# Agent attention with a max-out layer: keys and queries transposed by DMA, SBUF to SBUF, instead of by TensorE and VectorE

## The chip, the cores and the metric

The kernel runs on one core of a Trainium2 chip. The metric is device microseconds (us) of one execution. Shapes: q, k and v are 4 x 12544 x 128 in float32, the agents are 4 x 49 x 128, the output is 50176 x 128 in float32.

## The reference

```python
scale = 1.0 / np.sqrt(q.shape[-1])
def sm(a, b):
    s = scale * (a @ b.transpose(0, 2, 1))
    s = s - s.max(-1, keepdims=True)
    e = np.exp(s)
    return e / (e.sum(-1, keepdims=True) + 1e-09)
agent_v = sm(agents, k) @ v              # 49 x 128 for each batch
x = (sm(q, agents) @ agent_v)            # 12544 x 128 for each batch
x = x.reshape(B * S, D)
h = np.maximum(np.maximum(x @ w1, x @ w2), x @ w3)   # 768 hidden columns
out = h @ w_out
```

## The kernel before, in words

A batch has 12544 rows, cut into 13 groups: twelve of 8 x 128 rows and one of 2 x 128. Row t0 + p·n + j of a group lies on partition p, column block j. Every group of every batch is worked twice: once as a **k group** (keys and values, which build the agent values), and, when all k groups of its batch are done, as a **q group** (queries, hidden layer, output). The k groups of batch b+1 run beside the q groups of batch b; the k groups of batch 0 run alone at the start, and the q groups of batch 3 alone at the end.

**A k group.** `load` (L141) brings k and v in, 512 KB each, by two DMAs on the SP queue. `cast` (L148) turns both to bf16 on POOL (v on ACT in batch 0). `transposes` (L157) turns eight 128x128 blocks of keys on TensorE into the PSUM tile `m_ps`, and `evacuate` (L162) copies that to SBUF as `kT` on VectorE. `scores` (L166) multiplies `kT` by the agents, `exps` (L173) takes the exponential on ACT, `values` (L177) multiplies by the values and by ones, `accumulate` (L187) adds the result to `Eacc` on VectorE. After the last group `k_tail` (L207) normalises and multiplies by the three weight matrices, so that the hidden layer later takes the exponentials of the queries directly.

**A q group.** `load`, `cast`, `transposes` (L256), `evacuate` (L263) as above, with `qT` as result; `scores` (L267) and `exps` (L273) give the exponentials `e_q`. Then for each f of six slices of 128 hidden columns: `first` (L303) multiplies one weight difference, `relu_first` (L306) applies ReLU on ACT (into `a_sb`, or in place for the last slice, L309), `second` (L314) multiplies the other, and `max_second` (L317) takes the maximum of both on VectorE (L323; ACT for the last slice, L321). Products go to PSUM tiles `uv_ps`, of which there are three. `out_linear` (L325) and `out_hidden` (L332) form the output in PSUM (`o_ps`), `out_scale` (L340, line L344) divides by the sums of the exponentials on VectorE, and `store` (L349) writes it out on the SP queue.

**PSUM.** `uv_ps` takes six banks, `o_ps` one, `m_ps` one. All of the transposes, scores, values, sums and the products of `k_tail` go through that one `m_ps` bank, one after the other.

**Order.** The order is written by hand. Each step of a group is put down by `at(key + offset, step)`, six units of key being one group; all steps are sorted by key and issued in that order, and each engine and each DMA queue works in that order. So in the middle batches one turn of six units holds one k group and one q group of every stage. Of the steps that the change touches:

```python
        at(key - 20, load)         # k and q groups
        at(key - 12, cast)
        at(key - 0.6, transposes)  # k group, with key counted one group later
        at(key - 0.1, evacuate)
        at(key + 0.65, scores)
        at(key - 3.0, transposes)  # q group
        at(key - 2.6, evacuate)
        at(key - 1.75, scores)
```

SP's queue holds all large transfers: loads of q, k and v and the store, in the order of their keys; a waiting store holds up the loads behind it.

Of the kernel before, what the change touches and what calls it, by code (L numbers as in the profile page):

```python
# [10 lines left out]
BF16 = mybir.dt.bfloat16  # L11
# [5 lines left out]
def kernel(  # L17
# [18 lines left out]
    nc = tc.nc  # L36
    B, N, C = q.shape
    A = agents.shape[1]
    Dff = moe_w1.shape[1]
    scale = 1.0 / math.sqrt(C)  # L40
    P = 128
    NF = Dff // P
    H = 64
    GT = 8
# [5 lines left out]
    NG = len(sizes)  # L50
# [4 lines left out]
    work = ctx.enter_context(tc.tile_pool(name="work", bufs=2))  # L55
# [8 lines left out]
    def m_tile(dtype=FP32):  # L64
        return psum.tile([P, 512 if dtype == FP32 else 1024], dtype, tag="m", bufs=1, name="m_ps")
# [3 lines left out]
    def at(key, fn):  # L69
        ops.append((key, len(ops), fn))  # L70


    ident = const.tile([P, P], BF16, name="ident")
# [3 lines left out]
    agT = const.tile([P, B, H], BF16, name="agT")  # L77
# [9 lines left out]
    for i, w in enumerate((moe_w1, moe_w2, moe_w3)):  # L87
        t = const.tile([P, Dff], FP32, name=f"wst{i}")
# [42 lines left out]
    LEAD = 1  # L131
# [4 lines left out]
    def k_group(b, g):  # L136
        n, t0 = sizes[g], starts[g] * P
        key = 6.0 * (NG * (b - 1) + g - LEAD)
        d = {}

        def load():  # L141
            for name, src in (("k", k), ("v", v)):
                t = loads.tile([P, GT, C], FP32, tag=f"{name}_st", bufs=3, name=f"{name}_st")
                nc.sync.dma_start(t[:, :n, :],
                                  src[b, t0:t0 + n * P, :].rearrange("(p j) c -> p j c", j=n))
                d[name] = t

        def cast():  # L148
            d["kb"] = work.tile([P, GT, C], BF16, tag="k_bf", name="k_bf")
            nc.gpsimd.tensor_copy(out=d["kb"][:, :n, :], in_=d["k"][:, :n, :])  # L150
            d["vb"] = work.tile([P, GT, C], BF16, tag="v_bf", bufs=3, name="v_bf")
            if b == 0:
                nc.scalar.activation(d["vb"][:, :n, :], d["v"][:, :n, :], AF.Copy)
            else:
                nc.gpsimd.tensor_copy(out=d["vb"][:, :n, :], in_=d["v"][:, :n, :])  # L155

        def transposes():  # L157
            t = d["kT_ps"] = m_tile(BF16)
            for j in range(n):
                nc.tensor.transpose(t[:, j * P:(j + 1) * P], d["kb"][:, j, :], ident)  # L160

        def evacuate():  # L162
            d["kT"] = work.tile([P, GT * P], BF16, tag="kT", name="kT")
            nc.vector.tensor_copy(out=d["kT"][:, :n * P], in_=d["kT_ps"][:, :n * P])  # L164

        def scores():  # L166
            t = d["s"] = m_tile()
            sumtile["t"] = t
            for j in range(n):
                nc.tensor.matmul(t[:, j * A:(j + 1) * A], d["kT"][:, j * P:(j + 1) * P], agT[:, b, :A],  # L170
                                 start=(j == 0), stop=True, skip_group_check=True)

        def exps():  # L173
            d["e"] = work.tile([P, GT * A], BF16, tag="e_k", name="e_k")
            nc.scalar.activation(d["e"][:, :n * A], d["s"][:, :n * A], AF.Exp, scale=scale)  # L175

        def values():  # L177
            t = d["s"]
            c = GT * A
            for j in range(n):  # L180
                e = d["e"][:, j * A:(j + 1) * A]
                nc.tensor.matmul(t[:, c:c + A], d["vb"][:, j, :], e, start=False, stop=True,  # L182
                                 skip_group_check=True)
                nc.tensor.matmul(t[:, c + A:c + 2 * A], ones, e, start=False, stop=True,  # L184
                                 skip_group_check=True)

        def accumulate():  # L187
            c = GT * A
            if g == 0:
                Eacc[b] = work.tile([P, 2 * A], FP32, tag="Eacc", name="Eacc")  # L190
                nc.vector.tensor_copy(out=Eacc[b], in_=d["s"][:, c:c + 2 * A])
            else:
                nc.vector.tensor_tensor(out=Eacc[b], in0=d["s"][:, c:c + 2 * A], in1=Eacc[b],  # L193
                                        op=ALU.add)

        at(key - 20, load)
        at(key - 12, cast)
        at(key - 0.6, transposes)
        at(key - 0.1, evacuate)
        at(key + 0.65, scores)  # L200
        at(key + 1.35, exps)
        at(key + 2.3, values)
        at(key + 2.75, accumulate)
        if g == NG - 1:
            k_tail(b, key + 2.8)

    def k_tail(b, key):  # L207
        d = {}

        def normalise():  # L210
            E = Eacc[b]
            r = work.tile([P, A], FP32, tag="k_recip", name="k_recip")
            nc.vector.reciprocal(r, E[:, A:2 * A])
            d["avT"] = work.tile([P, H], BF16, tag="avT", name="avT")
            nc.vector.memset(d["avT"], 0.0)
            nc.vector.tensor_tensor(out=d["avT"][:, :A], in0=E[:, :A], in1=r, op=ALU.mult)
            G[b] = work.tile([P, WC], BF16, tag="G", name="G")

        def product(i):
            c0, c1 = i * 512, min((i + 1) * 512, WC)  # L220
            t = m_tile()
            for h in range(2):

                c = c0 + (C if c0 >= C1O and h == 0 else 0)
                nc.tensor.matmul(t[h * H:(h + 1) * H, :c1 - c0], d["avT"], wall[:, c:c + c1 - c0],  # L225
                                 start=True, stop=True, skip_group_check=True)
            if i % 2:
                nc.vector.tensor_copy(out=G[b][:, c0:c1], in_=t[:, :c1 - c0])
            else:
                nc.scalar.activation(G[b][:, c0:c1], t[:, :c1 - c0], AF.Copy)  # L230

        at(key, normalise)
        for i in range(-(-WC // 512)):
            at(key + 0.02 * (i + 1), lambda i=i: product(i))


    def q_group(b, g):
        n, t0 = sizes[g], starts[g] * P
        nh = n // 2
        T = nh * P  # L240
        pairs = [range(0, min(2, nh)), range(2, nh)]
        key = 6.0 * (NG * b + g)
        d = {}
# [10 lines left out]
            nc.gpsimd.tensor_copy(out=d["qb"][:, :n, :], in_=d["q"][:, :n, :])  # L254

        def transposes():  # L256
            t = d["qT_ps"] = m_tile(BF16)
            for j in range(n):
                jj, h = divmod(j, 2)
                i = h * nh + jj  # L260
                nc.tensor.transpose(t[:, i * P:(i + 1) * P], d["qb"][:, j, :], ident)  # L261

        def evacuate():  # L263
            d["qT"] = work.tile([P, GT * P], BF16, tag="qT", name="qT")
            nc.vector.tensor_copy(out=d["qT"][:, :n * P], in_=d["qT_ps"][:, :n * P])  # L265

        def scores():  # L267
            t = d["s"] = m_tile()
            for h in range(2):
                nc.tensor.matmul(t[h * H:(h + 1) * H, :T], agT[:, b, :], d["qT"][:, h * T:(h + 1) * T],  # L270
                                 start=True, stop=True, skip_group_check=True)

        def exps():  # L273
# [77 lines left out]
            nc.sync.dma_start(out[row:row + n * P, :].rearrange("(p j) c -> p j c", j=n),  # L351
                              d["out"][:, :n, :])

        at(key - 20, load)
        at(key - 12, cast)
        at(key - 3.0, transposes)
        at(key - 2.6, evacuate)
        at(key - 1.75, scores)
        at(key - 1.3, exps)
        at(key + 2.05, sums)  # L360
# [16 lines left out]
            at(e + scaled, lambda o=o: out_scale(o))  # L377
        at(e + 6.3, store)

    at(-6.0 * (NG + LEAD) - 21, prep)  # L380
    at(-6.0 * (NG + LEAD) + 12, prep_weights)
    for b in range(B):
        for g in range(NG):
            k_group(b, g)
            q_group(b, g)
# [34 lines left out]
```

## Time and profile before

| | us |
|---|---|
| median of 3 runs | 686.89 |
| lowest and highest of them | 685.15, 694.22 |
| the profiled execution's own time | 681.0 |
| its span, first to last instruction | 679.2 |

The span is the stretch in which instructions run; 1.8 us of the execution lie around it. Times in the trace count from its start. An engine's busy time is a sum over its instructions; whether it bounds a stretch is read from the waits there. In the rows PE is TensorE's matmul side, PEld its weight loads, DVE is VectorE, ACT ScalarE, POOL GpSimd, and SPq the queue of DMA issues on SyncE. Three stretches have a different make-up: the k groups of batch 0 alone (to about 70 us), the three batches with k and q groups, and batch 3's q groups alone (from about 540 us).

### The profile page before, as it was taken

How to read it: one execution, taken by the hardware profiler on the slowest of the kernel's cores; microseconds unless marked ns; L12 is line 12 of the kernel's file. 1: busy time of each engine (PE TensorE's matmuls, PEld its weight loads, DVE VectorE, ACT ScalarE, POOL GpSimd, SP SyncE). 2: the span in 40 equal slices, each digit the busy share in tenths (PEclk: the TensorE clock that was granted, in tenths of full speed). 3: DMA queues.
4: the chain of work that ended last, by engine and by line, in shares of the span. 5: the costliest groups of instructions: out<-in, count | busy, mean ns of one | idle time of the engine just before them, and what ended most of it. 6: DMA issues, size and time to landing. Idle time of an engine off the chain costs nothing.

```text
span 679.2 us, 14666 instructions
## 1 busy us (share of the span) xinstructions
PE 524.7 (77%) x6104; PEld 324.2 (48%) x6104; DVE 446.0 (66%) x603; ACT 416.8 (61%) x493; POOL 140.3 (21%) x149
## 2 busy tenths in 40 slices
PE   1555498888887778888888778888888778888886
PEld 1444245545544445554554445455555444555454
DVE  1322267676767478676778467677777467877875
ACT  2332166767676376767667366766667467777774
POOL 2123332322212132222213122222310011101000
PEclk9999999999999699999999699999999699999999
DMA  9767723463536273364445283354312131322111
GB/s 338 260 252 274 268 86 126 147 226 125 177 128 217 91 288 126 126 225 149 149 155 188 95 293 128 145 199 174 119 63 101 63 126 63 125 94 94 71 64 71
DMA packets 31438, 105.39 MB, mean 155 GB/s; under 512 B 3399, under 2 KB 6411, under 8 KB 31371
## 3 DMA queue, kind: packets, MB, share of 16 engines
q1 hardware_dynamic: 29952, 102.77, 42.3%
q10 hardware_dynamic: 1419, 1.67, 0.7%
q8 instruction: 48, 0.79, 0.5%
q14 instruction: 19, 0.16, 0.1%
HBM read 78.74 MB, written 25.69 MB: 154 GB/s over the span
## 4 chain that ended last, share of the span: by engine, by line
PE 56%; DVE 17%; ACT 10%; issue 6%; DVEq 0%; POOL 0%; ACTq 0%
PE o_ps L337 19%; PE uv_ps L298 17%; ACT a_sb L312 8%; DVE r L323 7%; PE o_ps L328 5%; DVE o_sb L344 5%; PE m_ps L261 5%; PE m_ps L160 3%; PE m_ps L270 2%; DVE kT L164 2%; DVE recips L290 1%; PE m_ps L182 1%; PE m_ps L225 1%; PE m_ps L184 1%; PE m_ps L170 1%
## 5 line engine op out<-in xcount | busy, mean ns | idle before, releaser
L312 ACT ACTIVATE a_sb<-uv_ps 128x1024 bf16<-128x1024 f32 (+1 forms) x260 | 251.3, 974 | 113.1 <-PE uv_ps L298 110.3
L323 DVE TENSOR_TENSOR r<-uv_ps,a_sb 128x1024 bf16<-128x1024 f32 (+1 forms) x260 | 295.0, 1157 | 26.5 <-PE uv_ps L298 17.8
L298 PE MATMUL uv_ps<-e_q,G 49*128 49x512 bf16 (+1 forms) x1248 | 212.8, 383 | 54.3 <-ACT a_sb L312 44.1
L337 PE MATMUL o_ps<-wo_bf,r 128*128 128x128 bf16 x2352 | 179.1, 224 | 0.0
L337 PEld LDWEIGHTS <-r 128*128 128x128 bf16 x2352 | 140.5, 100 | 53.4 <-issue 50.8
L298 PEld LDWEIGHTS <-G 49*128 49x128 bf16 x1248 | 60.1, 94 | 119.8 <-issue 84.0
L254 POOL CAST q_bf<-q_st 128x1024 bf16<-128x1024 f32 (+1 forms) x52 | 51.6, 993 | 299.7 <-issue 174.7
L164 DVE COPY kT<-m_ps 128x1024 bf16<-128x1024 bf16 (+1 forms) x52 | 34.4, 661 | 100.7 <-PE m_ps L160 100.7
L150 POOL CAST k_bf<-k_st 128x1024 bf16<-128x1024 f32 (+1 forms) x52 | 51.6, 992 | 203.8 <-PE m_ps L160 186.6
L344 DVE TENSOR_TENSOR o_sb<-o_ps,recips 128x512 f32<-128x512 f32 (+1 forms) x100 | 66.7, 667 | 27.4 <-PE o_ps L337 27.4
L309 ACT ACTIVATE uv_ps<-uv_ps 128x1024 f32<-128x1024 f32 (+1 forms) x52 | 49.9, 959 | 28.0 <-DVE r L323 23.4
L328 PE MATMUL o_ps<-G,e_q 128*128 128x256 bf16 x196 | 39.7, 283 | 32.1 <-DVE o_sb L344 32.1
L321 ACT ACTIVATE r<-uv_ps 128x1024 bf16<-128x1024 f32 (+1 forms) x52 | 50.7, 975 | 17.9 <-PE uv_ps L298 17.8
L175 ACT ACTIVATE e_k<-m_ps 128x392 bf16<-128x392 f32 (+1 forms) x52 | 24.9, 479 | 53.5 <-PE m_ps L170 53.2
L182 PE MATMUL m_ps<-e_k,v_bf 128*128 128x49 bf16 x392 | 30.5, 194 | 15.7 <-ACT e_k L175 15.7
L328 PEld LDWEIGHTS <-e_q 128*128 128x128 bf16 x196 | 12.3, 97 | 62.6 <-DVE o_sb L344 44.0
L160 PE MATMUL m_ps<-ident,k_bf 128*128 128x128 bf16 x392 | 37.5, 250 | 6.0 <-DVE Eacc L193 4.1
L265 DVE COPY qT<-m_ps 128x1024 bf16<-128x1024 bf16 (+1 forms) x52 | 34.3, 660 | 11.2 <-PE m_ps L261 9.8
L155 POOL CAST v_bf<-v_st 128x1024 bf16<-128x1024 f32 (+1 forms) x39 | 38.8, 994 | 0.0
L261 PE MATMUL m_ps<-ident,q_bf 128*128 128x128 bf16 x392 | 31.3, 223 | 9.3 <-DVE Eacc L193 6.2
L261 PEld LDWEIGHTS <-q_bf 128*128 128x128 bf16 x392 | 24.2, 99 | 22.4 <-issue 21.3
L160 PEld LDWEIGHTS <-k_bf 128*128 128x128 bf16 x392 | 30.2, 113 | 8.7 <-issue 8.6
(49 smaller groups left out, 269.6 us busy)
## 6 DMA issues: line engine op xcount, KB each, us to landing
k_st<-in_k_dram SPq DMA_DIRECT2D x48, 512.0 KB, 5.3
v_st<-in_v_dram SPq DMA_DIRECT2D x48, 512.0 KB, 5.8
q_st<-in_q_dram SPq DMA_DIRECT2D x48, 512.0 KB, 4.4
out_dram<-o_sb SPq DMA_DIRECT2D x48, 512.0 KB, 3.0
wst<-in_moe_w_dram ACTq DMA_DIRECT2D x3, 384.0 KB, 8.3
k_st<-in_k_dram SPq DMA_DIRECT2D x4, 128.0 KB, 4.2
v_st<-in_v_dram SPq DMA_DIRECT2D x4, 128.0 KB, 3.6
q_st<-in_q_dram SPq DMA_DIRECT2D x4, 128.0 KB, 2.8
```

The source lines that it names most:

```text
L150: nc.gpsimd.tensor_copy(out=d["kb"][:, :n, :], in_=d["k"][:, :n, :])
L160: nc.tensor.transpose(t[:, j * P:(j + 1) * P], d["kb"][:, j, :], ident)
L254: nc.gpsimd.tensor_copy(out=d["qb"][:, :n, :], in_=d["q"][:, :n, :])
L261: nc.tensor.transpose(t[:, i * P:(i + 1) * P], d["qb"][:, j, :], ident)
L298: nc.tensor.matmul(t[:, h, :T], G[b][h * H:h * H + A, col + f * P:col + (f + 1) * P], d["e"][h * H:h * H + A, :T], start=start, stop=True, ...
L309: nc.scalar.activation(u, u, AF.Relu)
L312: nc.scalar.activation(a_sb[f][:, :, :T], u, AF.Relu)
L321: nc.scalar.activation(r[:, :, :T], u, AF.Relu)
L323: nc.vector.tensor_tensor(out=r[:, :, :T], in0=u, in1=a_sb[f][:, :, :T], op=ALU.max)
L328: nc.tensor.matmul(t[:, i * 2 * C:(i + 1) * 2 * C], d["e"][:, jj * P:(jj + 1) * P], G[b][:, C1O:C1O + 2 * C], start=(i == 0), stop=False, ...
L337: nc.tensor.matmul(t[:, c:c + C], r_sb[f][:, h, jj * P:(jj + 1) * P], wo_bf[:, f, :], start=False, stop=(f == NF - 1), skip_group_check=True)
L344: nc.vector.tensor_tensor(out=d["out"][:, j:j + m, :], in0=d["o", o][:, :m * C].rearrange("p (j c) -> p j c", c=C), in1=d["r"][:, j:j + m] ...
```

## The change

The sixteen TensorE transposes of a full k and q group, and the two copies out of PSUM, go away. In their place stands one DMA transpose for each group, issued on the SP queue, which reads the bf16 keys (or queries) in SBUF and writes them transposed into SBUF, eight blocks of 128x128 by one instruction. `kT` and `qT` get three buffers in place of two. Loads are issued four units earlier, casts two; the transposes stand 8.2 (keys) and 10.2 units (queries) ahead of the group's key. The transposed queries lie in the order of the blocks, and the scores pick every second block.

```diff
@@ k_group @@
         def transposes():
-            t = d["kT_ps"] = m_tile(BF16)
-            for j in range(n):
-                nc.tensor.transpose(t[:, j * P:(j + 1) * P], d["kb"][:, j, :], ident)
-
-        def evacuate():
-            d["kT"] = work.tile([P, GT * P], BF16, tag="kT", name="kT")
-            nc.vector.tensor_copy(out=d["kT"][:, :n * P], in_=d["kT_ps"][:, :n * P])
+            d["kT"] = work.tile([P, GT, P], BF16, tag="kT", bufs=3, name="kT")
+            nc.sync.dma_start_transpose(out=d["kT"][:, :n, :],
+                                        in_=d["kb"][:, :n, :].rearrange("p j c -> p (j c)"))
...
-                nc.tensor.matmul(t[:, j * A:(j + 1) * A], d["kT"][:, j * P:(j + 1) * P], agT[:, b, :A],
+                nc.tensor.matmul(t[:, j * A:(j + 1) * A], d["kT"][:, j, :], agT[:, b, :A],
...
-        at(key - 20, load)
-        at(key - 12, cast)
-        at(key - 0.6, transposes)
-        at(key - 0.1, evacuate)
+        at(key - 24, load)
+        at(key - 14, cast)
+        at(key - 8.2, transposes)
@@ q_group @@
         def transposes():
-            t = d["qT_ps"] = m_tile(BF16)
-            for j in range(n):
-                jj, h = divmod(j, 2)
-                i = h * nh + jj
-                nc.tensor.transpose(t[:, i * P:(i + 1) * P], d["qb"][:, j, :], ident)
-
-        def evacuate():
-            d["qT"] = work.tile([P, GT * P], BF16, tag="qT", name="qT")
-            nc.vector.tensor_copy(out=d["qT"][:, :n * P], in_=d["qT_ps"][:, :n * P])
+            d["qT"] = work.tile([P, GT, P], BF16, tag="qT", bufs=3, name="qT")
+            nc.sync.dma_start_transpose(out=d["qT"][:, :n, :],
+                                        in_=d["qb"][:, :n, :].rearrange("p j c -> p (j c)"))
...
-                nc.tensor.matmul(t[h * H:(h + 1) * H, :T], agT[:, b, :], d["qT"][:, h * T:(h + 1) * T],
+                nc.tensor.matmul(t[h * H:(h + 1) * H, :T], agT[:, b, :], d["qT"][:, h:n:2, :],
...
-        at(key - 20, load)
-        at(key - 12, cast)
-        at(key - 3.0, transposes)
-        at(key - 2.6, evacuate)
+        at(key - 24, load)
+        at(key - 14, cast)
+        at(key - 10.2, transposes)
...
-    at(-6.0 * (NG + LEAD) - 21, prep)
+    at(-6.0 * (NG + LEAD) - 25, prep)
```

On VectorE, one turn of a middle batch of the kernel before: `recips` and `Eacc` close the sums, `o_sb` scales one half of an output, `qT` and `kT` are the copies out of PSUM, and the `r` are maxima of the hidden layer.

```order
L290 RECIPROCAL recips<-m_ps 128x8
L193 TENSOR_TENSOR Eacc<-m_ps,Eacc 128x98
L344 TENSOR_TENSOR o_sb<-o_ps,recips 128x512
L265 COPY qT<-m_ps 128x1024
L323 TENSOR_TENSOR r_4831<-uv_ps,a_sb 128x1024
L323 TENSOR_TENSOR r_4865<-uv_ps,a_sb 128x1024
L164 COPY kT<-m_ps 128x1024
L344 TENSOR_TENSOR o_sb<-o_ps,recips 128x512
```

On VectorE, the same stretch of the kernel after, where L279, L189, L333 and L312 are the lines that were L290, L193, L344 and L323.

```order
L279 RECIPROCAL recips<-m_ps 128x8
L189 TENSOR_TENSOR Eacc<-m_ps,Eacc 128x98
L333 TENSOR_TENSOR o_sb<-o_ps,recips 128x512
L312 TENSOR_TENSOR r_4499<-uv_ps,a_sb 128x1024
L312 TENSOR_TENSOR r_4535<-uv_ps,a_sb 128x1024
L333 TENSOR_TENSOR o_sb<-o_ps,recips 128x512
```

The two copies are gone, and nothing else has moved; TensorE's order likewise is the one before without the sixteen transposes.

On SP's queue, one turn of a middle batch before: the store, then the three loads, each with the semaphores that it waits for (DMAHW: an earlier transfer).

```order
L351 DMA out_dram<-o_sb 128x1024 [waits DMAHW7_49,DVE_49]
L250 DMA q_st<-in_q_dram 128x1024 [waits DMAHW0_49,Pool_49]
L144 DMA k_st<-in_k_dram 128x1024 [waits DMAHW1_49,Pool_49]
L144 DMA v_st<-in_v_dram 128x1024 [waits DMAHW2_49,Pool_49]
L351 DMA out_dram<-o_sb 128x1024 [waits DMAHW3_49,DVE_49]
```

On SP's queue, one turn of a middle batch after: L340 is the store, L253 and L159 are the DMA transposes of queries and keys, L245 and L144 the loads.

```order
L340 DMA out_dram<-o_sb 128x1024 [waits DMAHW2_49,DVE_49]
L253 DMA_TRANSPOSE qT<-q_bf 128x8x128 [waits DMAHW3_49,PE_49,Pool_49]
L159 DMA_TRANSPOSE kT<-k_bf 128x8x128 [waits DMAHW4_49,PE_49,Pool_49]
L245 DMA q_st<-in_q_dram 128x1024 [waits DMAHW5_49]
L144 DMA k_st<-in_k_dram 128x1024 [waits DMAHW6_49]
L144 DMA v_st<-in_v_dram 128x1024 [waits DMAHW7_49,Pool_49]
L340 DMA out_dram<-o_sb 128x1024 [waits DMAHW0_49,DVE_49]
```

Both transposes now stand between the store and the loads, and the loads wait behind them.

## Rows read from the trace of the kernel before

**Rows 1.** The page, part 1: busy us, share of the span, instructions.
```profile
PE 524.7 (77%) x6104; PEld 324.2 (48%) x6104; DVE 446.0 (66%) x603; ACT 416.8 (61%) x493; POOL 140.3 (21%) x149
```

**Rows 2.** Stretches (us from:to): length, busy of each engine, clock, DMA share, GB/s.
```profile
103.14:208.48 105.34, 86.85 (x1100) 54.22 (x1098) 78.58 (x99) 72.40 (x82) 25.70 (x27) 1.00 0.45 160
311.70:323.40 11.70, 9.64 (x124) 6.02 (x123) 8.72 (x12) 8.04 (x10) 3.06 (x4) 1.00 0.51 181
602.67:612.76 10.09, 8.77 (x92) 5.16 (x90) 7.90 (x11) 7.45 (x9) 1.04 (x1) 1.00 0.31 110
```

**Rows 3.** Chain that ended last, 316 to 323 us: start, us, what.
```profile
316.17 0.61 PE m_ps L261 x8
316.77 0.34 PE uv_ps L298 x2
...
317.14 1.03 ACT a_sb L312
...
320.65 0.78 PE o_ps L337 x12
321.42 0.46 PE m_ps L160 x8
...
321.91 0.35 DVE kT L164
322.26 0.26 issue
322.52 0.69 DVE o_sb L344
```

**Rows 4.** Timeline, 315 to 319 and 617 to 619 us: start, us, engine, line, [idle before].
```profile
315.58 0.39 PE L298 MATMUL uv_ps<-e_q,G 49*128 49x512 bf16 x2
...
316.81 0.69 DVE L265 COPY qT<-m_ps 128x1024 bf16<-128x1024 bf16 x1 [0.19 <-PE m_ps L261]
...
317.42 2.34 DVE L323 TENSOR_TENSOR r<-uv_ps,a_sb 128x1024 bf16<-128x1024 f32 x2
...
318.69 1.01 ACT L309 ACTIVATE uv_ps<-uv_ps 128x1024 f32<-128x1024 f32 x1 [0.53 <-DVE r L323]
...
617.42 0.84 PE L337 MATMUL o_ps<-wo_bf,r 128*128 128x128 bf16 x12
...
618.30 0.69 DVE L344 TENSOR_TENSOR o_sb<-o_ps,recips 128x512 f32<-128x512 f32 x1 [1.70 <-PE o_ps L337]
```

**Rows 5.** Groups of instructions by form: busy us, mean ns, idle before.
```profile
L164 DVE COPY kT<-m_ps 128x1024 bf16<-128x1024 bf16 x48 | 33.2, 692 | 94.8 <-PE m_ps L160 94.8
L265 DVE COPY qT<-m_ps 128x1024 bf16<-128x1024 bf16 x48 | 33.2, 692 | 11.2 <-PE m_ps L261 9.8
```

**Rows 6.** DMA: queues of the first 20 us (packets, MB, share), issues of the whole.
```profile
q1 hardware_dynamic: 1422, 5.21, 68.5%
q10 hardware_dynamic: 1418, 1.67, 23.4%
...
q_st<-in_q_dram SPq DMA_DIRECT2D x48, 512.0 KB, 4.4
...
q_st<-in_q_dram SPq DMA_DIRECT2D x4, 128.0 KB, 2.8
```

**Rows 7.** Timeline of SP's queue, two issues of one turn: start, us.
```profile
311.96 0.39 SPq L250 DMA_DIRECT2D q_st<-in_q_dram  x1
...
312.44 0.74 SPq L144 DMA_DIRECT2D k_st<-in_k_dram  x1
```

**Rows 8.** Waits of SP's queue, longest in total: us, times, longest.
```profile
SPq L351 <- DVE o_sb L344: 444.6, 48, 22.6
```

**Rows 9.** Timeline of VectorE among batch 0's k groups: start, us, [idle before].
```profile
48.08 0.69 DVE L164 COPY kT<-m_ps 128x1024 bf16<-128x1024 bf16 x1 [1.10 <-PE m_ps L160]
...
52.27 0.69 DVE L164 COPY kT<-m_ps 128x1024 bf16<-128x1024 bf16 x1 [1.10 <-PE m_ps L160]
```

## The prediction

> **What bounds the kernel now.** I read the page's engine totals first. No engine is full: PE 77%, VectorE 66%, ACT 61% [rows 1]. So the time lies in waits between engines, and the next view is the stretches. The kernel repeats one turn (a k group and a q group). Nine turns of batch 0 take 105.34 us, that is 11.70 us each, and a turn of batch 3, which has no k group beside it, takes 10.09 [rows 2]. In the 11.70 us turn PE is busy 9.64, VectorE 8.72, ACT 8.04 us, so even the fullest idles for 2 us. DMA works 51% of that turn, TensorE is granted its full clock (1.00, the level of 2.4 GHz). The third view, the chain that ended last, says where the 11.70 go: a ring from PE to VectorE to ACT and back, and both transposes are links of it [rows 3]. The query transposes hold PE for 0.61 us, the next hidden product follows, then a ReLU on ACT. Later the key transposes hold PE for 0.46, VectorE copies `kT`, and only behind that copy comes `o_sb`, which frees the output bank for the next products.
>
> **What goes.** Query side, per turn. The hidden products at 315.58 (0.39 for two) are the last before the transposes; the next ones start at 316.77 in the chain, after L261 [rows 3, 4]. Without L261 they can follow at about 315.8 to 315.9, so the ReLU of 317.14 moves forward by 0.9. VectorE, which copies `qT` from 316.81 and starts its maxima at 317.42 [rows 4], starts them when the copy's place is empty, 0.8 earlier (0.61 of the copy's 0.69, since instructions overlap, and the idle 0.19 ahead of it). ACT's L309 waits for the first of these maxima [rows 4]. The later of the two counts: 0.8 us.
>
> Key side, per turn. `o_sb` needs the products that end at 321.43 (320.65 + 0.78), but starts at 322.52, after the key transposes, the copy and 0.26 of issue [rows 3]. How it looks without keys stands in batch 3: there L337 ends at 618.26 and `o_sb` starts at 618.30 [rows 4]. So 322.52 becomes 321.47: 1.05 us.
>
> Together 1.85 us, and the turn falls to 9.85. That is still above each engine's work: VectorE 8.72 - 2 x 0.69 = 7.34 [rows 2, 5], ACT 8.04, PE about 8.6. A cross-check from the other batch: 10.09 less the 0.8 of the query side is 9.3; in the 11.70 turn the k group cost 1.61 more than in batch 3, 1.05 of it the part that now goes, which leaves 0.56, and 9.3 + 0.56 = 9.86.
>
> **What comes, first the bytes.** No transpose by DMA stands in the trace, so its price is bounded from rows. A full group moves 256 KB in and out. In the first 20 us the large packets took 0.685 x 20 x 16 / 1422 = 0.154 us of one DMA engine for 3.66 KB, the others 0.234 x 320 / 1418 = 0.053 us for 1.18 KB [rows 6]: an estimate of 0.005 us a packet and 0.041 us a KB (1000 bytes). With 4096-byte packets the 64 packets of a transpose cost 0.7 us of all 16 engines; with 256-byte packets (128 bf16 of one row, the runs of the source) 1024 cost 1.0 us; with 32-byte packets 3.1 us; with two-byte ones 39 us. I take 1.0, the source's own runs. Two in a turn add 2.0 to the 0.51 x 11.70 = 6.0 us that DMA works now [rows 2]: 8.0 of 9.85, hidden. It stays hidden up to 1.9 us a transpose, and eats the whole gain at 2.9.
>
> **Then the queue.** SP holds a plain transfer 0.39 to 0.74 us [rows 7], four of them about 1.9 in a turn, and else waits for `o_sb` (444.6 us in all, [rows 8]). I take an issue like theirs, 0.7, for a transpose; SP has room for (9.85 - 1.9) / 2 = 4.0 each. The three loads now stand behind two transposes, which wait for POOL's casts; the casts stand 3.8 units (6.2 us) and 5.8 units (9.5 us) ahead of them, and POOL works 3.06 us in a turn [rows 2], so this wait is hidden. The scores stand 8.45 units (13.9 us) behind the transposes of the queries and 8.85 (14.5 us) behind those of the keys; a 512 KB load lands in 4.4 us at the median [rows 6]. Each transposed tile has three buffers, so the landing has more than a turn before anybody waits.
>
> A rule weighed against this: the Trainium skill ("Advanced Engine Details and Errata", X-Bar Transpose) says that transposing DMAs are as fast as ordinary ones on this chip; with its 350 to 400 GB/s a transpose would take an estimated 0.7 us, and the sum would be the same as above. No run here shows it yet.
>
> **The start.** In batch 0's k groups a group takes 52.27 - 48.08 = 4.19 us [rows 9], 1.1 of it VectorE waiting for the key transposes. Removing them could bring a megabyte of loads to its DMA pace, near 3 us; but each group gets a transpose on the queue and 2.8 us or more of landing [rows 6] ahead of its scores. Between 15 us saved and 15 us lost I take 0.
>
> **The sum.** 27 turns (nine in batch 0, the three middle batches being alike) x 1.85 = 50. The other 11 turns with a k group, at the ends of batches with the short group and `k_tail`, between 0.8 and 1.85, say 1.2: 13. Twelve turns of batch 3 x 0.8 = 10. Start 0. Together 73 us off the profiled execution's 681.0: 608. The median of the runs shown is 5.9 above that execution, so the forecast for a median is **614 us**; by itself it would lie between 596 and 645 (gain between 90, with a faster start, and 42, about 60% of the links).
>
> **Rivals.** *The transposes cannot keep the pace.* Two of them share SP's queue in each turn. If they run one after the other and take more than 11.70 / 2 = 5.85 us each, the scores wait for them in every turn, and the kernel is slower than before: that is the point from which it decides. The rows give from one landing, 1.0 + 2.8 = 3.8 us, to one landing for each of the eight blocks, 22.4 [rows 6]. Their middle in ratio is 9.2: 39 turns with k groups x 18.4 = 718, 13 of batch 3 at 9.3 = 121, 13 k groups at the start x 9.2 = 120, **about 960 us**. For it speaks that the work is cut into small pieces and all on one queue; against it that each plain transfer uses all 16 engines and overlaps with its neighbours. It starts gently: at 6.5 us each it is about 710. By the Trainium skill ("VectorE: DVE Perf Modes", The three transpose paths) one 128x128 block takes 1309 ns by DMA and 390 by TensorE; eight blocks in a row would be an estimated 10.5 us, and this rival's sum 39 x 20.9 + 13 x 10.5 x 2 = 1090. That rule speaks against the change, and nothing in the trace of before decides between it and the one above.
>
> *The cover is only partly there.* DMA work of 2 to 3 us a transpose, or SP held for about 4.5: the turn becomes 10.9 to 11.7 and the start some us longer, **about 670 us**. Thirty-two-byte writes would be this case. For it speaks that DMA is already at 51% of the turn [rows 2], and at 68.5 + 23.4 = 92% in the first 20 us [rows 6].
>
> *The links are replaced.* VectorE's maxima and ACT's ReLUs hold the ring anyway, and only the key side goes, less what is late next: 0.6 a turn over 38 turns, **about 655 us**. For it speaks that between the links the ring alternates ACT and VectorE with the three `uv_ps` tiles; against it batch 3, where the key side is really absent and the turn is 1.6 shorter.
>
> That the change does not do what it says is not open: no transpose of keys or queries is left on TensorE, and the copies are gone.
>
> **How the numbers follow.** Forecast 0.47; pace 0.34; partial cover 0.13; replaced links 0.06. A measurement of this kernel can tell about 2% (14 us) from no change. Faster by more: 0.47 + 0.06 + the best sixth of partial cover (0.02) = 0.55. Within 2%: most of partial cover, 0.08. Slower: 0.34 + 0.03 of partial cover that runs over = 0.37. The range must leave out no more than 2 in 10: below 596 some 0.05, and of the pace case (which reaches from 700 past 1090) the upper part, 0.15, so it goes to 930.
>
> **What would show it.** Right: no wait of the scores for `kT` or `qT`, a turn of 9.7 to 10.2 in the middle batches and 9.2 to 9.5 in batch 3, `o_sb` starting straight after L326's products, DMA share near 0.8 in a turn, transposes landing in under 8 us. Wrong: TensorE's scores (L166, L259) or POOL's casts waiting for DMA in every turn, SP held longer than 4 us by one transpose, a landing of over 10 us, the loads issued late behind the transposes, or batch 3 and the middle batches falling to the same length only because the queue sets both.

## The result, and the profile after

The kernel after takes 603.43 us (median of four runs, 602.93 to 606.06) against 686.02 before: ratio 0.8784, 95% interval 0.8708 to 0.8859. The forecast was 614, with 596 to 645 as its own range. The profiled execution went from 681.0 to 602.93 us; the prediction took 73 us off, 78 went.

The page of the kernel after: engine totals, the large queue, and the DMA transposes with their median landing (us).

```profile
PE 471.4 (78%) x5320; PEld 285.2 (47%) x5320; DVE 383.8 (64%) x499; ACT 412.5 (69%) x493; POOL 140.3 (23%) x149
...
q1 hardware_dynamic: 133632, 128.48, 76.7%
...
kT<-k_bf SPq DMA_TRANSPOSE x52, 5.2
qT<-q_bf SPq DMA_TRANSPOSE x52, 4.5
```

Against [rows 1], PE lost 53 us of work and VectorE 62, and still no engine is full. The queue has 103680 packets more than the 29952 of the page before, about a thousand for each full transpose.

Stretches of the kernel after (from:to, length, PE, PEld, DVE, ACT, POOL busy, clock, DMA share, GB/s): seven turns and a single turn of middle batches, one late in batch 2 when no more keys are loaded, a turn of batch 3, and two turns where the clock is low.

```profile
98.73:166.88 68.15, 59.34 (x744) 37.58 (x742) 52.74 (x64) 55.17 (x64) 19.58 (x22) 1.00 1.00 257
...
262.54:272.28 9.74, 8.48 (x108) 5.37 (x106) 7.54 (x10) 7.88 (x10) 3.02 (x4) 1.00 0.90 249
433.20:442.94 9.74, 8.48 (x108) 5.38 (x108) 7.54 (x10) 7.89 (x10) 1.73 (x2) 1.00 0.49 152
566.65:576.08 9.43, 8.23 (x84) 4.63 (x82) 7.21 (x9) 7.44 (x9) 0.00 (x0) 1.00 0.19 64
...
546.45:557.23 10.78, 9.60 (x84) 5.13 (x82) 7.20 (x10) 7.53 (x9) 1.04 (x1) 0.84 0.28 78
...
209.38:221.31 11.93, 9.67 (x82) 5.44 (x81) 6.60 (x9) 8.21 (x10) 3.08 (x4) 0.68 1.09 299
```

These answer to [rows 2]. The middle turn fell from 11.70 to 9.74 us, seven in a row in the first line (68.15 / 7); batch 3's from 10.09 to 9.43. The DMA share of the first two lines is 1.00 and 0.90, where it was 0.51 (packets in flight together count each, so a share can pass 1). In the third line it is 0.49, and the turn is 9.74 all the same: the ring sets the pace, not the queue. The last two lines are turns with TensorE's clock at 0.84 and 0.68, partly at its lower level of 1.2 GHz; they come back below.

Timeline of the kernel after in one turn (start, us, [idle before]), which answers to [rows 3, 4, 7].

```profile
137.56 0.82 PE L287 MATMUL uv_ps<-e_q,G 49*128 49x512 bf16 x6
...
137.92 0.68 DVE L333 TENSOR_TENSOR o_sb<-o_ps,recips 128x512 f32<-128x512 f32 x1
...
138.52 2.35 DVE L312 TENSOR_TENSOR r<-uv_ps,a_sb 128x1024 bf16<-128x1024 f32 x2
...
141.65 0.84 PE L326 MATMUL o_ps<-wo_bf,r 128*128 128x128 bf16 x12
...
142.53 0.69 DVE L333 TENSOR_TENSOR o_sb<-o_ps,recips 128x512 f32<-128x512 f32 x1 [1.67 <-PE o_ps L326]
...
143.70 1.47 SPq L253 DMA_TRANSPOSE qT<-q_bf  x1
...
145.27 1.46 SPq L159 DMA_TRANSPOSE kT<-k_bf  x1
```

Both links are gone as forecast. The six hidden products run in one piece, where L261 stood between two and four; VectorE goes from one output half straight into its maxima; and `o_sb` starts 0.04 us after the products end (141.65 + 0.84 = 142.49), as in batch 3 before.

Waits of the kernel after (who waited for whom: us in total, times, longest).

```profile
POOL q_bf L249 <- DMA qT<-q_bf: 150.0, 26, 16.1
...
PE m_ps L166 <- DMA kT<-k_bf: 24.4, 10, 10.2
...
PE m_ps L259 <- DMA qT<-q_bf: 0.9, 1, 0.9
```

The long new wait is POOL's, for one of its two `q_bf` buffers to be read out by a transpose, in 26 of 52 casts. The query scores behind these casts waited once, 0.9 us in all, so it costs nothing. The key scores waited ten times, 10.2 of the 24.4 us in one go, and all ten lie before 60 us, among the k groups of batch 0: in the middle turns neither kind of scores waits.

Timeline of VectorE in the start (k groups of batch 0) of the kernel after; the last line is the same step of the kernel before.

```profile
54.37 0.26 DVE L189 TENSOR_TENSOR Eacc<-m_ps,Eacc 128x98 f32<-128x98 f32 x1 [2.80 <-PE m_ps L180]
57.93 0.26 DVE L189 TENSOR_TENSOR Eacc<-m_ps,Eacc 128x98 f32<-128x98 f32 x1 [3.31 <-PE m_ps L180]
61.07 0.26 DVE L189 TENSOR_TENSOR Eacc<-m_ps,Eacc 128x98 f32<-128x98 f32 x1 [2.88 <-PE m_ps L180]
61.37 0.47 DVE L208 RECIPROCAL k_recip<-Eacc 128x49 f32<-128x49 f32 x1
...
70.11 0.47 DVE L213 RECIPROCAL k_recip<-Eacc 128x49 f32<-128x49 f32 x1
```

A k group takes 3.1 to 3.6 us here, against 4.19 in [rows 9], though its scores now wait 1.1 to 2.2 us for a transpose to land (the first of all 10.2). The last one is added at 61.1 us, and the normalising begins at 61.37, before at 70.11.

### The profile page after: what moved, and what is told of

The parts are those of the page before. It is cut to its first block, busy times and chain, and to the rows that moved or that the text cites. A ratio compares the mean times of both kernels' runs of the same rounds, so it can differ in the third digit from the quotient of the medians.

```text
span 601.1 us, 13157 instructions
## 1 busy us (share of the span) xinstructions
PE 471.4 (78%) x5320; PEld 285.2 (47%) x5320; DVE 383.8 (64%) x499; ACT 412.5 (69%) x493; POOL 140.3 (23%) x149
## 4 chain that ended last, share of the span: by engine, by line
PE 49%; ACT 18%; DVE 15%; DMA 9%; issue 6%; SPq 1%; POOL 1%; ACTq 0%; POOLq 0%; DVEq 0%
PE uv_ps L287 20%; PE o_ps L326 18%; ACT a_sb L301 14%; DVE r L312 12%; DMA kT<-k_bf 6%; PE o_ps L317 4%; PE m_ps L259 3%; DVE o_sb L333 3%; ACT r L310 2%; DMA qT<-q_bf 1%; PE m_ps L178 1%; PE m_ps L180 1%; DMA wst<-in_moe_w_dram 1%; PE m_ps L220 1%; POOL k_bf L150 1%
## 5 line engine op out<-in xcount | busy, mean ns | idle before, releaser
L312 DVE TENSOR_TENSOR r<-uv_ps,a_sb 128x1024 bf16<-128x1024 f32 (+1 forms) x260 | 295.0, 1158 | 40.7 <-ACT a_sb L301 27.7
L301 ACT ACTIVATE a_sb<-uv_ps 128x1024 bf16<-128x1024 f32 (+1 forms) x260 | 248.3, 975 | 71.7 <-PE uv_ps L287 69.9
L326 PE MATMUL o_ps<-wo_bf,r 128*128 128x128 bf16 x2352 | 184.1, 227 | 0.0
L326 PEld LDWEIGHTS <-r 128*128 128x128 bf16 x2352 | 144.4, 101 | 52.0 <-issue 49.2
L287 PEld LDWEIGHTS <-G 49*128 49x128 bf16 x1248 | 65.5, 95 | 131.8 <-issue 93.4
L333 DVE TENSOR_TENSOR o_sb<-o_ps,recips 128x512 f32<-128x512 f32 (+1 forms) x100 | 67.0, 670 | 95.1 <-PE o_ps L326 95.1
L166 PE MATMUL m_ps<-agT,kT 128*128 128x49 bf16 x392 | 20.9, 196 | 25.7 <-DMA kT<-k_bf 24.4
L189 DVE TENSOR_TENSOR Eacc<-m_ps,Eacc 128x98 f32<-128x98 f32 x48 | 10.6, 221 | 35.7 <-PE m_ps L180 35.7
L264 ACT ACTIVATE e_q<-m_ps 128x512 bf16<-128x512 f32 (+1 forms) x52 | 29.5, 568 | 3.7 <-PE m_ps L259 3.6
L180 PE MATMUL m_ps<-e_k,ones 128*128 128x49 bf16 x392 | 30.9, 194 | 0.0
L180 PEld LDWEIGHTS <-ones 128*128 128x128 bf16 x392 | 26.0, 103 | 10.0 <-issue 10.0
L166 PEld LDWEIGHTS <-kT 128*128 128x128 bf16 x392 | 17.3, 104 | 28.3 <-DMA kT<-k_bf 25.7
```

The lines of the kernel that those rows point to most:

```text
L287: nc.tensor.matmul(t[:, h, :T], G[b][h * H:h * H + A, col + f * P:col + (f + 1) * P], d["e"][h * H:h * H + A, :T], start=start, stop=True, ...
L301: nc.scalar.activation(a_sb[f][:, :, :T], u, AF.Relu)
L312: nc.vector.tensor_tensor(out=r[:, :, :T], in0=u, in1=a_sb[f][:, :, :T], op=ALU.max)
L326: nc.tensor.matmul(t[:, c:c + C], r_sb[f][:, h, jj * P:(jj + 1) * P], wo_bf[:, f, :], start=False, stop=(f == NF - 1), skip_group_check=True)
L333: nc.vector.tensor_tensor(out=d["out"][:, j:j + m, :], in0=d["o", o][:, :m * C].rearrange("p (j c) -> p j c", c=C), in1=d["r"][:, j:j + m] ...
```

## The experiments

**One side at a time.** The kernel after with its q group, or its k group, as in the kernel before (the places of the steps; the comments stand for what `transposes` does, and its code, not shown, is that of the same kernel):

```diff
@@ keys only: q_group @@
-        at(key - 24, load)
-        at(key - 14, cast)
-        at(key - 10.2, transposes)      # DMA
+        at(key - 20, load)
+        at(key - 12, cast)
+        at(key - 3.0, transposes)       # TensorE
+        at(key - 2.6, evacuate)
@@ queries only: k_group @@
-        at(key - 24, load)
-        at(key - 14, cast)
-        at(key - 8.2, transposes)       # DMA
+        at(key - 20, load)
+        at(key - 12, cast)
+        at(key - 0.6, transposes)       # TensorE
+        at(key - 0.1, evacuate)
```

> Keys are transposed by DMA as in the kernel after, queries by TensorE and VectorE with the keys' and queries' own offsets of the two kernels. Theory (two separate links, each worth its own stretch of the chain): the turn of the middle batches falls from 11.70 by the key side's 1.05 to about 10.65, batch 3 stays at 10.08, the start ends near 61 us as in the kernel after; in all about 636 us. Rival (one common link, so that either side alone brings most of it): the turn falls to about 10.0 or below, about 615 us. Rival (only both together bring anything): the turn stays at 11.4 or above, about 665 us.

> Queries are transposed by DMA as in the kernel after, keys by TensorE and VectorE. Theory (two separate links): the middle turn falls by the query side's 0.8 to about 10.9 and batch 3's to 9.43, the start stays at 70 us; in all about 650 us. Rival (one common link): about 10.0 a turn, 620 us. Rival (only both together): 11.4 or above, 670 us.

Keys only: 644.89 us, ratio 0.9384 (0.9341 to 0.9426). Two `recips` one turn apart in a middle batch:

```profile
289.24 0.21 DVE L285 RECIPROCAL recips<-m_ps 128x8 f32<-128x8 f32 x1 [0.25 <-PE m_ps L180]
299.89 0.21 DVE L285 RECIPROCAL recips<-m_ps 128x8 f32<-128x8 f32 x1 [0.25 <-PE m_ps L180]
```

Queries only: 644.15 us, ratio 0.9376 (0.9326 to 0.9426). One turn of a middle batch, then one of batch 3:

```profile
288.65 0.21 DVE L284 RECIPROCAL recips<-m_ps 128x8 f32<-128x8 f32 x1 [0.24 <-PE m_ps L184]
299.44 0.21 DVE L284 RECIPROCAL recips<-m_ps 128x8 f32<-128x8 f32 x1 [0.24 <-PE m_ps L184]
...
606.79 0.20 DVE L284 RECIPROCAL recips<-m_ps 128x8 f32<-128x8 f32 x1
616.22 0.20 DVE L284 RECIPROCAL recips<-m_ps 128x8 f32<-128x8 f32 x1
```

The turns are 10.65 and 10.79: 1.05 us for the keys, 0.91 for the queries, and 11.70 - 1.05 - 0.91 = 9.74, the turn of the kernel after. Two separate links, which add up; both rivals fall, the common link and the gain that needs both sides. The start ended at 60.7 us with keys only and at 70.0 with queries only, so its gain is the keys' as well. The totals were less well foretold than the turns (636 and 650): keys only lost some 2 us in the first full turns of each later batch, at clocks of 0.71 and 0.72. The third buffer of `kT` and `qT` was not tested by itself. In [rows 5] all of the wait of the `kT` copies, and 9.8 of 11.2 us of the `qT` copies', is for the transposes on TensorE, so a lack of buffers is not what held them.

**The earlier loads alone.**

```diff
@@ kernel before, k_group and q_group @@
-        at(key - 20, load)
-        at(key - 12, cast)
+        at(key - 24, load)
+        at(key - 14, cast)
...
-    at(-6.0 * (NG + LEAD) - 21, prep)
+    at(-6.0 * (NG + LEAD) - 25, prep)
```

> The kernel before with the loads, casts and the first step placed earlier as in the kernel after; all transposes on TensorE. Theory (the gain is the links that went, not the earlier loads): 681 to 689 us, no change, turn 11.70, since no wait of the middle turns ends with a load. Rival (a part of the gain is the earlier loads and casts): 10 us or more faster.

686.2 us, ratio 1.0004 (0.9958 to 1.0051), turn 11.70. The lead brings nothing by itself.

**Every transpose twice.**

```diff
@@ k_group, and the same in q_group @@
             nc.sync.dma_start_transpose(out=d["kT"][:, :n, :], ...
+            again = work.tile([P, GT, P], BF16, tag="kT2", bufs=2, name="kT2")
+            nc.sync.dma_start_transpose(out=again[:, :n, :], ...
```

> The kernel after with every DMA transpose issued twice, the second into a tile that nobody reads. Theory (a transpose costs about 1.8 us of all 16 DMA engines, from the growth of the queue's share, and the turn of after is just below what DMA can bear): a turn needs 6.0 + 4 x 1.8 = 13.1 us of DMA, so DMA becomes the bound, turn about 13, batch 3 unchanged at 9.4, start about 85 us, in all about 740 us. Rival (1.0 us as predicted, and the larger share is only packets waiting for each other): 6.0 + 4.0 = 10.0, turn 9.8 to 10.2, about 615 us. Rival (SP's issue bounds: 1.5 to 3.9 us held by each transpose): turn 12 to 14 with the DMA share well below 1.

685.73 us (one run), about the time of the kernel before. Stretch of batch 1 (columns as above), and the wait of the query scores, which was 0.9 us in the kernel after:

```profile
236.36:385.98 149.62, 121.30 (x1326) 73.55 (x1326) 94.21 (x122) 99.82 (x119) 37.98 (x39) 0.87 1.10 257
```

```profile
PE m_ps L265 <- DMA qT<-q_bf: 34.0, 17, 5.1
```

Of the first expectation, the start (its normalising begins at 86.0 us) and batch 3's turn (9.43) came true, the middle turn and the total did not; of the two rivals nothing did. Some turns stayed at 9.74 and others went to 12 to 16, at clocks of 0.75 to 0.87, so a part of what they lost may be the clock's.

Batch 1 has twelve full groups and one of a quarter, so a full group took 149.62 / 12.25 = 12.2 us. Had DMA worked without a pause, a transpose would cost (12.2 - 6.0) / 4 = 1.55 us there, an estimate from above that lies between the two prices. That the transfers now come too late is shown by the 17 waits of the query scores; the share of 1.10 alone doesn't show it, since turns of 9.74 us in the kernel after have such shares too. At its shortest holds SP would need some 7 us a turn for four transposes and four plain transfers, which speaks for the DMA engines as the bound, but the two were not told apart. The run also gives the distance to the edge: twice the transposes eat the whole gain.

**The transpose by itself.** The order of the transfers, in outline:

```diff
+        for i in range(24):
+            turn(...)                # DMA transpose of one 256 KB tile
+        for i in range(24):
+            load(i, ...)             # plain load of 512 KB, after the last transpose
+        for i in range(24):
+            load(24 + i, ...)
+            turn()
```

> No attention and no hidden layer: one query group is loaded and cast, then 24 DMA transposes of 256 KB, then 24 plain loads of 512 KB, then 24 of each in turn; the output is one stored tile. Theory (a transpose costs the 16 engines about 1.4 us, from the 11.6 us mean turn of the run with every transpose doubled: (11.6 - 6.0) / 4): 34 us for the transposes, about 35 for the loads, 69 for both mixed. Rival (1.0 us, the prediction's term): 24, 35 and 59 us. Rival (transposes and loads disturb each other): the mixed stretch is over 10% longer than the sum of the two before it.

One run. Stretches (length, DVE, POOL busy, clock, DMA share, GB/s): transposes, loads, both.

```profile
10.93:46.17 35.24, 0.15 (x1) 0.00 (x0) 1.00 0.95 179
46.17:81.21 35.04, 0.15 (x1) 0.00 (x0) 1.00 0.94 359
81.21:146.10 64.89, 0.15 (x1) 0.00 (x0) 1.00 1.10 290
```

The issues of its transposes on SP's queue (ns, min/median/max):

```profile
L385 SPq DMA_TRANSPOSE qT<-q_bf x49: 1232/1344/2807, 6.1 to 141.5; - x49
```

A transpose takes 35.24 / 24 = 1.47 us, a load of twice its bytes 1.46: half the rate in bytes, 179 against 359 GB/s. Mixed, a pair takes 2.70, 8% less than apart, so they don't disturb each other; if a load keeps its 1.46 there, an estimated 1.24 are left for the transpose. SP is held for 1.23 us or more by each, 1.34 at the median, nearly the 1.47 itself, and for up to 2.8 with loads between; whether the DMA engines or the issue set the pace here stays open.

**Where the query side's 0.91 us comes from.**

```diff
@@ kernel after, q_group @@
+        def unread():
+            t = m_tile(BF16)
+            for j in range(n):
+                nc.tensor.transpose(t[:, j * P:(j + 1) * P], d["qb"][:, j, :], ident)
+        at(key - 3.0, unread)
```

> The kernel after with the queries' TensorE transposes put back at their old place, into an m_ps tile that nobody reads; no copy on VectorE. Theory (the query side's 0.90 us is TensorE's part: the next hidden products come behind the transposes, and the ReLU behind them): turn 10.6, batch 3 about 10.1, in all about 645 us. Rival (it is VectorE's copy, which pushes the maxima that ACT's L298 waits for, as the prediction's 0.8 had it): turn 9.75 to 9.95, about 608 us.

623.01 us (one run). One turn of a middle batch, and one of batch 3:

```profile
281.79 0.21 DVE L286 RECIPROCAL recips<-m_ps 128x8 f32<-128x8 f32 x1 [0.20 <-PE m_ps L180]
291.97 0.21 DVE L286 RECIPROCAL recips<-m_ps 128x8 f32<-128x8 f32 x1 [0.20 <-PE m_ps L180]
...
566.14 0.20 DVE L286 RECIPROCAL recips<-m_ps 128x8 f32<-128x8 f32 x1
575.87 0.20 DVE L286 RECIPROCAL recips<-m_ps 128x8 f32<-128x8 f32 x1
```

Neither of the two expectations: 10.18 and 9.73, that is 0.44 and 0.30 more than without. About half of the link is TensorE's transposes; the other half, by difference, is the copy on VectorE behind them, which no run put back alone.

**The clock.** The kernel after, on the same chip as the next run, repeated at 604.6 us, ratio 0.8815 (0.8776 to 0.8855).

> The kernel after, unchanged, on the chip of the runs beside it: 602 to 606 us.

To that kernel two matmuls of constants were added, where TensorE waits 0.9 us in most turns:

```diff
@@ kernel after, q_group @@
+        def fill():
+            t = m_tile()
+            for _ in range(2):
+                nc.tensor.matmul(t[:, :512], ones, wall[:, :512], start=True, stop=True,
+                                 skip_group_check=True)
+        at(key + 4.02, fill)
```

> The kernel after with two 128x512 matmuls more in each q group, of constants, into a fresh m_ps tile that nobody reads, at the place where TensorE waits 0.9 us for a ReLU (before L287's last slice). Theory (TensorE's clock falls to its half level more often than before the change because the transposes no longer fill such gaps): the drops inside batch 3 go, its slow turns of 10.8 to 10.9 become 9.43, the mean granted clock rises from 0.948 to 0.965 or more, and the whole falls by 4 to 10 us against the kernel after. Rival (the drops have another cause, or the filler adds a link to the ring): clock as in the kernel after, the turn 9.74 or longer, 603 to 620 us.

593.92 us, ratio 0.8653 (0.8622 to 0.8683), 1.8% below the kernel after. The filler and the slice behind it on PE, then mean clock and two stretches, the first full turn of batch 1 and a turn of batch 3, and last the first full turn of batch 1 in the repeat of the kernel after.

```profile
269.94 0.60 PE L358 MATMUL m_ps<-wall,ones 128*128 128x512 bf16 x2
270.90 0.39 PE L287 MATMUL uv_ps<-e_q,G 49*128 49x512 bf16 x2 [0.36 <-ACT a_sb L301]
```

```profile
core 0: 592.5 us, clock 0.974
```

```profile
211.02:220.43 9.41, 7.52 (x84) 4.18 (x83) 6.50 (x9) 8.04 (x10) 3.06 (x3) 1.00 1.09 267
...
510.80:520.30 9.50, 9.01 (x86) 4.86 (x86) 7.27 (x10) 7.67 (x9) 1.04 (x1) 1.00 0.50 141
...
211.28:221.74 10.46, 8.20 (x82) 4.51 (x81) 6.60 (x10) 8.15 (x10) 3.01 (x4) 0.84 1.09 292
```

The middle turn is 9.74 as before, so the filler adds no link: PE still waits 0.36 us behind it. What changed is the clock. The first full turn of batch 1 took 11.93 us at 0.68 in the first profile of the kernel after and 10.46 at 0.84 in its repeat; it takes 9.41 at 1.00 here. Of the turns of 10.7 to 10.9 us in the later part of batch 3, two in either profile, none is left.

How such a fall looks on PE in the kernel after, at 214 us, and a wait of that kernel (us in total, times, longest):

```profile
210.99 0.39 PE L287 MATMUL uv_ps<-e_q,G 49*128 49x512 bf16 x2 [0.89 <-ACT a_sb L301]
...
212.52 1.11 PE L287 MATMUL uv_ps<-e_q,G 49*128 49x512 bf16 x6 [0.81 <-ACT uv_ps L298]
214.09 0.61 PE L287 MATMUL uv_ps<-e_q,G 49*128 49x512 bf16 x2 [0.45 <-ACT r L310]
```

```profile
PE uv_ps L287 <- ACT a_sb L301: 43.6, 52, 0.9
```

TensorE had worked in short pieces, with waits of 0.45 to 0.89 us between them; then two products take 0.61 in place of 0.39. The wait of 0.9 us by itself doesn't bring a fall, since it stands in most turns; what decides was not found.

The same filler in the kernel before, as a control, and a longer one at the head of `k_tail`:

```diff
@@ kernel with the filler, k_tail @@
+        at(key + 0.01, fill)     # five such matmuls, while the values are normalised
```

> The kernel before with the same two matmuls in each q group at the same place, transposes on TensorE. Theory (the filler pays back a loss that the change itself brought, since in the kernel before the transposes keep TensorE busy through most turns and the clock is 0.975): no change beyond 2 us, 683 to 688. Rival (the filler is a gain of its own, with or without the change): 4 us or more faster than the kernel before.

> The run with the filler, and five more 128x512 matmuls of constants into a fresh m_ps tile at the head of k_tail, where TensorE waits about 1.2 us for the normalised agent values; nobody reads them. Theory (the half clock at the ends of batches comes from those waits too): the clock in the stretch at the end of a batch rises above 0.8, and the whole falls by a further 2 to 8 us against 593.9. Rival (the later waits of k_tail for its copies are what counts, or the filler holds up the products): 593 to 600 us, clock at the ends of batches as in the run with the filler.

The control took 679.92 us, ratio 0.9874 (0.9801 to 0.9947), small but clear of 1, at a clock of 0.982, where the runs of the kernel before beside it had 0.946 to 0.965. So the filler is a gain of its own, if a smaller one: the rival of that run holds, and only the rest, 1.8% against 1.3%, can be the change's doing, which is less than the intervals tell apart. The filler at `k_tail` raised the clock at the end of batch 0 (187 to 203 us) from 0.79 to 0.89, but the whole came to 593.67, ratio 0.8621 (0.856 to 0.8682): no gain that can be told from the run without it. The kernel after with the filler is the fastest that was clearly shown, 593.92 us.

## Why the prediction was right, point by point

**The ring.** Right, and the main reason: the gain was read from the waits of one turn, not from engine totals. The key side was forecast at 1.05 us and measured 1.05: it was read off batch 3, where a turn without keys already stood in the trace. The query side was forecast at 0.8 and measured 0.91. The step that was off is "The later of the two counts": the transposes on TensorE and the copy on VectorE did not hide each other but cost about 0.45 each, the second by difference. A turn of 9.85 became 9.74; batch 3's 9.3 became 9.43.

**The sum.** The 27 turns gave 51 us (50 forecast): 1.96 each, but nothing from one that a low clock kept at 11.82. The start, put at 0 between 15 either way, gave 8.7. Batch 3 gave 3.2 in place of 10: 0.65 in the plain turns, less what slow-clock turns of 10.8 to 10.9 us and a longer first stretch took back. The other turns and the ends of batches give the remaining 15, where 13 was forecast, though made up differently: their first turns were partly longer than before, at clocks of 0.68 to 0.84. That 78 came so close to 73 is partly luck: the start, for which nothing was put down, made up for what batch 3 missed. And half of the 10.6 us between 614 and the median is the 5.9 by which the forecast set a median above its profiled execution; after the change that distance is 0.5.

**The price of a transpose.** Mis-sized, though inside the bounds. The packets were right: 256-byte runs, 1024 for each (103680 more in the queue, all of them under 512 bytes). The price of one was not: 1.0 us of all engines was forecast, 1.47 measured alone; mixed with loads it is an estimated 1.24, and in the doubled run at most an estimated 1.55. SP is held 1.2 us at least and 1.5 at the median, where 0.7 was taken. The cover was there but thinner than written: 6.0 + 2 x 1.47 = 8.9 of 9.74, and a DMA share of 0.82 to 1.17 in the turns of 9.74 us while all loads run, where "near 0.8" was named. The edge computed from rows, 1.9 us a transpose for a free ride and 2.9 for none, fits the doubled run: two transposes of 1.47 are 2.9 for each one needed, and the gain was gone. Two signs that the prediction had named for being wrong did show, each in part, and cost the middle turns nothing: half of POOL's query casts wait for a transpose, and one transpose, at 72 us, held SP for 5.1 us.

**The rivals.** The pace case did not come: landing is 5.2 and 4.5 us at the median, 8.5 at most, and neither kind of scores waits in the middle turns. The per-block price of the Trainium skill ("VectorE: DVE Perf Modes", The three transpose paths), 1309 ns, does not add up over the blocks of one instruction: eight took 1.47 us, 0.18 each. The other rule of the Trainium skill ("Advanced Engine Details and Errata", X-Bar Transpose) has transposes as fast as ordinary DMAs, at 350 to 400 GB/s. The run of transposes alone does not agree: 179 GB/s, half of the plain 359. That the links are replaced fell with the two one-sided runs. The partial cover came near: the doubled run is about what it describes.

## What to carry to other kernels

When transposes and their copies are links of a ring between engines, look for a stretch of the same kernel where one of them is missing: its turn prices the link better than a sum of durations did here. A DMA transpose is worth it while the DMA engines have room: here 256 KB took 1.47 us alone, as much as a plain load of twice the bytes, and 1.2 to 1.5 us of the issuing queue. Look at TensorE's granted clock turn by turn, and at what a few matmuls of constants do in its waits.

## What the runs showed of the hardware that was not expected

Two matmuls on constants that nobody reads, placed in a wait of 0.9 us, made the kernel after 1.8% faster and the kernel before 1.3%: the mean granted clock rose from 0.946 to 0.974 in the one. A transpose and a load on one queue, mixed, took 2.70 us, 8% less than the 2.93 of one after the other.
